# Queries and keys turned on TensorE in 64x64 array tiles in place of DMA transposes

## The chip, the cores and the metric

The kernel runs on one core of one Trainium2 chip, in one launch. The metric is the device time in microseconds (us) of one execution; the comparison uses the median of several runs. Each kernel also has one profiled execution, whose span is counted from the first to the last instruction of the program.

## The reference

An attention with normalised queries and keys, and behind it a chain of matrix products on its output. In short:

```python
# q, k, v: (8, 12, 448, 64) float32; g_q, g_k: (64,)
q_n = q / sqrt(mean(q * q) + 1e-6) * g_q        # over the last axis; k likewise with g_k
s   = (q_n @ k_n.T) / sqrt(64)
s   = s - max(s)
p   = exp(s); p = p / (sum(p) + 1e-9)
x   = (p @ v), as 3584 tokens x 768             # 8 batches x 448 tokens, 12 heads x 64
a   = x @ w1; b = x @ w2                        # w1, w2: 768 x 1024
out = ((a * b) @ w3) @ w_out                    # w3: 1024 x 1024, w_out: 1024 x 768
```

## The kernel before

**Tiling.** The work is cut into 24 *quads*: a quad is four heads of one batch, so three quads make a batch. Tokens are split as 64 x 7, so that a loaded tile has 128 partitions (two groups of 64 rows) and seven blocks `j` on the free axis. `w3 @ w_out` is formed once on the chip (`w34s`), so the chain behind the attention has two stages: FFN1 (`x` times `w1` and `w2`, multiplied together) and FFN2 (times `w34s`).

**One quad, in order.** `load_qk` brings queries and keys in (L384). `plan_prep` squares them on ScalarE (L487), sums the squares on VectorE (L492), takes the inverse root on ScalarE (L501 and L504) and scales them into the bf16 tile `qks` on VectorE (L526). Then `qks` has to be turned so that the head dimension lies on partitions, into `qkT`. That is done in two ways:

- For the first five quads (`N_PE_T = 5`) `do_turn` transposes the seven 128x128 blocks of one operand on TensorE (L1163) into one PSUM bank, and a copy on VectorE or ScalarE brings them to `qkT`; for queries the copy also multiplies by the gains `g_col`.
- For the 19 quads after these, `send` issues one DMA transpose for each operand on SP's queue (L600). When the queries have landed, VectorE multiplies them by the gains in place (`by_g`, L534).

`do_score` then multiplies keys and queries in 64x64 array tiles (L716), seven scores a quad of four matmuls each, every one followed by an exponential on ScalarE (L738). When two quads are complete their sums and values are formed together (`start_pv`; L782 for the left-over rows in 64x32 tiles, L803 for the rest in 128x32 tiles), and VectorE multiplies by the reciprocal of the sums (L845). Single quads take a longer form of the same. When three quads of a batch are done, the batch's FFN pairs join a list of waiting work. A pair (`do_pass`, L908) fills two PSUM banks with sums in 64x64 tiles, one pass of four matmuls at a time, and is emptied by VectorE or ScalarE. Half way through, the row halves of the array exchange banks; a nop on POOL or SP (`hand_over`, L892) stands between the halves. The last token tile is done in `do_last` (L1104).

**What sets the order.** The order of the instructions on every engine is computed when the program is built, by a small planner (`Planner`). It holds a list of jobs with estimated durations and needs, a model of the two DMA queues, and the time at which each PSUM bank comes free (`bank_at`). `pe_try` picks what TensorE does next: a value group, a turn (`any_turn`), a score, the running pair or a new one. Its thresholds are the constants at the top of the kernel (`PAIRS`, `MARGINS`, `LOWS`, `SOONS`, `STOCKS`, `PACES`, `AGAINST` and others; where there are two values, the second holds from `SWITCH = 55.0` on). On the chip the engines are kept in step by semaphores alone: the planner's times decide the order, not when something runs.

**Tile shapes.** The 64x64 tiles of scores and passes, the 128x128 of turns, the 64x32 and 128x32 of values are different settings of the array. The planner charges a change between them `DRAIN = 0.11` us (`into`).

**The start.** `WARM = 15` matmuls on an empty tile run while the first data arrive (L1360), and the planner fills TensorE's idle time up to `WARM_TO` with smaller ones (L1233).

Of the kernel before, what the change touches and what calls it, by code (L numbers as in the profile page):

```python
# [20 lines left out]
SEM = 0.05  # L21
# [5 lines left out]
AFTER = 0.7  # L27
LATE = 0.619
BUSY = 75.0

# [15 lines left out]
class Planner:  # L46
# [50 lines left out]
    def commit(self, job, start, engine):  # L97
        end = start + job.took[engine]
        self.free[engine] = end
        end += LAG[engine]  # L100
        self.jobs.remove(job)
        job.at = start
        if job.any:
            job.emit(engine)
        else:
            job.emit()
        if job.moves is not None:
            work, piece = job.moves
            ticket = [INF]
            self.landed[engine].append(ticket)  # L110

            def landed(t):
                self.note(job, t, engine)
                t += LATE if t > BUSY else 0.0
                ticket[0] = t
                if job.done:
                    job.done(t)

            self.moving[engine].append([start + AHEAD[engine], work, landed, piece])
        elif job.done:  # L120
            job.done(end)
# [74 lines left out]
def kernel(  # L196
# [41 lines left out]

    N_PE_T = 5
    QUAD = 13.122  # L240
    WARM = 15
    WARM_TO = 13.215
    WARM_N = 256
    PAIRS = (2, 3)
    MARGINS = (0.267, 0.281)
    LOWS = (0, 2)
    VALUE_BANKS = (6, 6)
    HOLD = 0
    SOONS = (2, 4)
    STARVES = (6, 5)  # L250
    HUNGERS = (0.632, 0.85)
    ONES = (0, 0)
# [4 lines left out]
    EARLY = 4  # L257
    STOCKS = (17, 14)
    PACES = (1.289, 1.754)
    SWITCH = 55.0  # L260
    LONGEST_SEND = 3.0
    SPLIT = 1
    SQUARE_ON_DVE = ([0, 0],)
    SCALE_ON_ACT = ()
    LATER = 12.232
    BY_G = 0.36
    KEYS = (1.8, 1.348)
    AGAINST = (68, 115, 120, 138, 154, 245, 257, 272, 278, 299, 308, 326)
    POOL_ORDER = (
# [5 lines left out]
    THIN_FROM = 9  # L275
    THIN = 0.627
    QUIET = 0.2

# [110 lines left out]
    def plan_load_qk(i, key=None):  # L389
        eng, queue = (nc.gpsimd, "POOL") if i in ON_POOL else (nc.sync, "SP")  # L390

        def thin():

            left = sum(x[1] for x in plan.moving["SP"])
            return 0.0 if i < THIN_FROM or left < THIN else INF

        parts = 2 if i in IN_PARTS else 1
        for which in range(2):
            got = []

            def done(t, which=which, got=got):
                got.append(t)
                landed[i]["qk"[which]] = all_of(got, parts)

            for n in range(parts):
                x0, x1 = 2 * n // parts, 2 * (n + 1) // parts
                add(
                    queue, {"SP": 0.4, "POOL": 0.75}[queue],
                    (quad(i) - 30 if key is None else key) + which * 0.01 + n * 0.001,
                    lambda which=which, x0=x0, x1=x1: load_qk(i, which, eng, x0, x1),  # L410
                    needs=[lambda: qk_free[i % 3] + (1.0 if i > 5 else 0.0), thin],
                    done=done, moves=(1.35 / parts, 0.086),
                )
# [19 lines left out]
    def plan_load_v(i, key, pieces=range(4)):  # L433
# [13 lines left out]
        for z in pieces:  # L447
            add(
                "POOL", 0.62, key + z * 0.01, lambda z=z: load_v(i, z),
                needs=[lambda: v_free[i % 4] + (3.0 if i > 3 else 0.0), quiet], done=done,  # L450
                moves=((0.46, 0.06), (0.38, 0.05))[z % 2],
            )
# [21 lines left out]
    def plan_prep(i):  # L474
        s = st[i]
        pe = i < N_PE_T
        key = quad(i)
# [54 lines left out]

        def by_g():
            nc.vector.tensor_scalar(  # L534
                out=s["qkT"][:, 0], in0=s["qkT"][:, 0], scalar1=g_col, scalar2=None,
                op0=MULT,
            )

        alpha_at = [INF, INF]
# [44 lines left out]

        def sent(t):
            def done(z):
                s["sent"][t] = z
                if t:
                    put(qkT_at[i], t)(z)
                else:  # L590
                    add(
                        "DVE", BY_G, key - 8, by_g, needs=[lambda: z + SEM],
                        done=put(qkT_at[i], t),
                    )

            return done

        def send(t):
            sent_at[0] = plan.now
            nc.sync.dma_start_transpose(  # L600
                out=s["qkT"][:, t], in_=s["qks"][:, t].rearrange("p j x d -> p (j x d)")
            )

        def complete(t, z):
            scaled_at[i][t] = z + SEM
            if max(scaled_at[i]) < INF and i + 3 < NQ:
                if i + 3 not in ON_POOL:
                    plan_load_qk(i + 3)
                plan_prep(i + 3)
            if not pe:  # L610
                add(
                    "SP", 1.3, key - 8 + t, lambda: send(t),
                    needs=[lambda: scaled_at[i][t]],
                    done=sent(t), moves=(1.6, 0.026),
                )

# [241 lines left out]
    pairs = []  # L858
    sent_at = [0.0]
    waiting = []  # L860
# [23 lines left out]
    def hand_over(p, mm, t):  # L884

        at = t + 0.23
        e = "POOL"
        if max(w_at["w2"]) == INF or (
            max(free["SP"], sent_at[0] + LONGEST_SEND) <= at and plan.moving["POOL"]
        ):  # L890
            e = "SP"
# [143 lines left out]
    def ffn2_pair(bp, t):  # L1035
        def evacuate(p, at):
# [13 lines left out]
            def copied(e):  # L1050
                freed(z)(e)
                for x in range(2):
                    if x and bp == B // 2 - 1:
# [6 lines left out]
                        "SP", 0.57, -20.0, lambda x=x: store(x),  # L1060
                        needs=[lambda: e + SEM], moves=(0.55, 0.14),
                    )
# [89 lines left out]

    turns = [(i, w) for i in range(N_PE_T) for w in range(2)]
    w3_turns = list(range(CF))

    def do_turn(t, i, w, z):
        s = st[i]
        ps = ps_all[:, z, :].bitcast(BF)[:, 0 : NJ * NP].rearrange(
            "p (j s) -> p j s", j=NJ
        )  # L1160
        took = into("t") + NJ * 0.067
        for j in range(NJ):
            nc.tensor.transpose(  # L1163
                ps[:, j], s["qks"][:, w, j].rearrange("p x d -> p (x d)"), ident
            )
        bank_at[z] = INF
        at = t + took + 0.18
        s["sent"][w] = at

        def done(e):  # L1170
            bank_at[z] = e + SEM
            qkT_at[i][w] = e

        add(
            None, {"DVE": 0.53, "ACT": 0.83}, -950.0 + i,
            lambda e: copy_on(e, s["qkT"][:, w], ps, None if w else g_col),
            needs=[lambda: at, lambda: consts_at["g"]], done=done,
# [30 lines left out]
    def any_turn(t, r, idle, n):  # L1208
# [3 lines left out]
        if turns:  # L1212
            i, w = turns[0]
            if scaled_at[i][w] <= r:
                turns.pop(0)
                return do_turn(t, i, w, single(idle))
        ready = [fc for fc in w3_turns if w_at["w3"][fc] + SEM <= r]
# [124 lines left out]
    with tc.manual_schedule():  # L1342
# [39 lines left out]

        warm(WARM)
        free.update(ACT=4.0, DVE=4.0, SP=4.0, POOL=2.3, PE=7.2)
        plan.now = plan.moved_to = 2.2
# [15 lines left out]
        def weight(emit, moves, done):  # L1401
            add("POOL", 0.6, -100.0 + seq[0], emit, done=done, moves=moves)

# [49 lines left out]
```

## Time and profile before

| | |
|---|---|
| median of three runs | 351.32 us (350.1 to 352.6) |
| the profiled execution | 349.81 us, of which the span is 348.0 us |
| granted TensorE clock, mean | 0.998 |
| TensorE busy | 342.3 us (98%), 7373 matmuls |
| TensorE weight loads busy | 219.3 us (63%) |
| VectorE busy | 206.7 us (59%) |
| ScalarE busy | 260.8 us (75%) |
| DMA transposes | 38 on SP's queue, median 4.0 us from issue to landing |
| gain passes at L534 | 19, 8.7 us together |
| turns at L1163 | 70 matmuls of 128x128 |

"PE" in the profile is TensorE's matmuls, "PEld" its weight loads, "DVE" VectorE, "ACT" ScalarE, "POOL" GpSimd and "SP" the engine that issues most DMAs. Matmuls are pipelined: one instruction's time is longer than the distance to the next one's start, so a busy TensorE is not a full one. The distance between starts tells what it is able to do. "Idle before" in the groups is the time that an engine stood still just before these instructions, and what ended it.

### The profile page before, as it was taken

The page shows a single profiled execution, that of the slowest core. Times are in us where ns is not written, and L with a number is a line of the kernel's source. Part 1 is how long each engine was busy: PE and PEld are TensorE (multiplying, and loading weights), DVE is VectorE, ACT ScalarE, POOL GpSimd, SP SyncE. Part 2 cuts the span into 40 slices and gives each one's busy share as a digit, 9 for nine tenths or more (in the row PEclk, how much of TensorE's full clock was granted, in tenths as well). Part 3 has the DMA queues.
Part 4 walks back from the last instruction along what each step waited for, and adds up shares of the span by engine and source line. Part 5 has one row for each costly group of instructions (what it writes and reads, how often), then busy time and mean ns, then how long its engine had stood idle before and what let it go on. Part 6 is the DMA issues. An engine that isn't in the chain of part 4 may idle for free.

```text
span 348.0 us, 16174 instructions
## 1 busy us (share of the span) xinstructions
PE 342.3 (98%) x7373; PEld 219.3 (63%) x7373; DVE 206.7 (59%) x296; ACT 260.8 (75%) x371; POOL 76.9 (22%) x134
## 2 busy tenths in 40 slices
PE   8999999999999999999999999999999999999995
PEld 4767756656775756566666575566665665666674
DVE  5369289898956687486567963865894313222100
ACT  4779989999997997998799797978987882222122
POOL 8556820302222301222022022212204000000000
PEclk9999999999999999999999999999999999999999
DMA  8999999499995969948898699477898051000055
GB/s 197 206 312 204 241 299 268 89 202 199 208 187 174 92 156 188 260 107 154 148 246 161 169 165 259 116 131 186 197 185 105 7 133 53 4 2 2 4 166 155
DMA packets 68488, 55.11 MB, mean 158 GB/s; under 512 B 45060, under 2 KB 62372, under 8 KB 68420
## 3 DMA queue, kind: packets, MB, share of 16 engines
q1 hardware_dynamic: 49440, 35.33, 43.0%
q0 software_dynamic: 18048, 16.92, 29.6%
q10 hardware_dynamic: 932, 1.84, 1.4%
q8 instruction: 57, 0.93, 1.1%
q14 instruction: 11, 0.09, 0.1%
HBM read 46.66 MB, written 11.01 MB: 166 GB/s over the span
## 4 chain that ended last, share of the span: by engine, by line
PE 98%; ACT 1%; DVE 0%; issue 0%
PE ps_all L908 68%; PE ps_all L803 13%; PE ps_all L716 9%; PE ps_all L782 2%; PE ps_all L1360 2%; PE ps_all L1163 1%; PE ps_all L1185 1%; PE ps_all L1104 1%; PE ps_all L1233 1%; ACT P L738 0%; DVE abT L989 0%; ACT qk_sb L369 0%; DVE warm_t L1343 0%; PE ps_all L1373 0%
## 5 line engine op out<-in xcount | busy, mean ns | idle before, releaser
L738 ACT ACTIVATE P<-ps_all 128x896 bf16<-128x896 f32 x114 | 99.5, 916 | 11.7 <-PE ps_all L716 10.8
L424 POOL DMA_DIRECT2D v_sb<-in_v_dram x96 | 57.3, 611 | 184.1 <-PE ps_all L716 120.3
L908 PE MATMUL ps_all<-xT,w2s 64*64 64x448 bf16 x1536 | 88.5, 349 | 0.0
L908 PE MATMUL ps_all<-xT,w1s 64*64 64x448 bf16 x1536 | 86.5, 349 | 0.0
L908 PE MATMUL ps_all<-w34s,abT 64*64 64x384 bf16 x1728 | 80.2, 323 | 0.4 <-DVE abT L989 0.4
L369 ACT ACTIVATE half<-ps_all 128x896 bf16<-128x896 f32 (+1 forms) x35 | 30.6, 874 | 48.5 <-PE ps_all L908 48.3
L908 PEld LDWEIGHTS <-abT 64*64 64x64 bf16 x1728 | 51.7, 107 | 20.3 <-issue 0.7
L908 PEld LDWEIGHTS <-w2s 64*64 64x64 bf16 x1536 | 46.5, 107 | 25.6
L908 PEld LDWEIGHTS <-w1s 64*64 64x64 bf16 x1536 | 46.0, 107 | 25.7 <-issue 0.4
L716 PE MATMUL ps_all<-qkT 64*64 64x448 bf16 x672 | 60.3, 351 | 0.0
L989 DVE TENSOR_TENSOR abT<-ps_all,half 128x896 bf16<-128x896 f32 x32 | 34.8, 1089 | 41.2 <-PE ps_all L908 41.1
L492 DVE TENSOR_REDUCE ssq<-sq 128x14 f32<-128x896 f32 (+1 forms) x50 | 51.2, 1041 | 12.5 <-ACT sq L487 12.2
L526 DVE TENSOR_TENSOR qks<-qk_sb,al 128x448 bf16<-128x448 f32 x96 | 54.6, 616 | 4.8 <-ACT al L504 4.7
L487 ACT ACTIVATE sq<-qk_sb 128x896 f32<-128x896 f32 (+1 forms) x50 | 45.1, 917 | 1.6 <-DMA qk_sb<-in_q_dram 1.3
L845 DVE TENSOR_TENSOR xT<-ps_all,r 128x448 bf16<-128x448 f32 x48 | 27.5, 618 | 25.6 <-ACT r L826 22.0
L716 PEld LDWEIGHTS <-qkT 64*64 64x64 bf16 x672 | 21.7, 106 | 13.2 <-issue 4.2
L908 PE MATMUL ps_all<-w_outs,w3T 64*64 64x384 bf16 x512 | 25.1, 324 | 0.1
L803 PE MATMUL ps_all<-P,v_sb 128*32 128x448 bf16 x456 | 25.0, 352 | 0.0
L738 ACT ACTIVATE w_outs<-ps_all 128x896 bf16<-128x896 f32 x24 | 21.4, 915 | 3.2 <-PE ps_all L716 3.0
L803 PEld LDWEIGHTS <-v_sb 128*32 128x32 bf16 x592 | 15.9, 97 | 12.2 <-issue 0.2
L738 ACT ACTIVATE Pr<-ps_all 128x896 bf16<-128x896 f32 x24 | 22.1, 920 | 0.6 <-PE ps_all L716 0.5
L375 DVE COPY half<-ps_all 128x768 f32<-128x768 f32 x13 | 12.4, 955 | 12.7 <-PE ps_all L908 12.7
(63 smaller groups left out, 210.9 us busy)
## 6 DMA issues: line engine op xcount, KB each, us to landing
out_dram<-half SPq DMA_DIRECT2D x48, 192.0 KB, 3.3
qk_sb<-in_q_dram SPq DMA_DIRECT2D x15, 448.0 KB, 6.3
qk_sb<-in_k_dram SPq DMA_DIRECT2D x15, 448.0 KB, 5.4
v_sb<-in_v_dram POOLq DMA_DIRECT2D x48, 64.0 KB, 4.0
v_sb<-in_v_dram POOLq DMA_DIRECT2D x48, 48.0 KB, 4.1
qk_sb<-in_q_dram POOLq DMA_DIRECT2D x5, 448.0 KB, 8.7
qk_sb<-in_k_dram POOLq DMA_DIRECT2D x5, 448.0 KB, 9.4
w3s<-in_moe_w_dram POOLq DMA_DIRECT2D x8, 256.0 KB, 6.8
```

What stands on the lines that cost most here:

```text
L369: nc.scalar.activation(out=out, in_=in_, func=AF.Copy, scale=1.0 if by is None else by)
L375: nc.vector.tensor_copy(out=out, in_=in_)
L424: nc.gpsimd.dma_start(out=v_bufs[i % 4][p0 : p0 + HP, g::2, 0 : j1 - j0].rearrange("p h j d -> p h (j d)"), in_=src[:, g::2, j0:j1].rearra ...
L487: nc.scalar.activation(out=out, in_=in_, func=AF.Square)
L492: nc.vector.tensor_reduce(out=s["ssq"][:, t, x0:x1], in_=s["sq", t][:, x0:x1], axis=AX, op=ADD)
L526: nc.vector.tensor_tensor(out=s["qks"][:, t, :, x], in0=src[:, t, x], in1=s["alpha"][:, t, x].unsqueeze(2).broadcast_to([NP, NJ, D]), op=MULT,
L716: nc.tensor.matmul(out=sc[HP * c : HP * c + HP, u, 0:S].rearrange("p (j s) -> p j s", j=NJ), lhsT=qkT[u * D : (u + 1) * D, 1, j, cols], rh ...
L738: lambda: nc.scalar.activation(out=dst, in_=sc[:, :, 0:S], func=AF.Exp),
L803: nc.tensor.matmul(out=ps_all[hd * HALF : (hd + 1) * HALF, z, 0:S], lhsT=value_weights(i, hd, j, kind), rhs=s["P"][:, hd, j, :] if j < NF ...
L845: lambda: nc.vector.tensor_tensor(out=xT[b][:, 2 * m + kind - 1, :], in0=ps, in1=s["r"], op=MULT),
L908: mm = nc.tensor.matmul(out=ps_all[64 * h : 64 * h + 64, p.bank + z, 0 : p.n], lhsT=lhsT[64 * r : 64 * r + 64, 64 * h : 64 * h + 64], rhs= ...
L989: nc.vector.tensor_tensor(out=abT[bp][:, f0 : f0 + 2, odd * S : (odd + 1) * S], in0=ps_all[:, z : z + 2, 0:S], in1=a_sb[b, f0], op=MULT,)
```

## The change

Every quad's operands are turned on TensorE. The first five quads (`SMALL_FROM = 5`, the same five) keep the 128x128 turn into one bank. The 19 after these take a turn in 64x64 array tiles: each 128x128 block is transposed as four 64x64 quarters, one on each tile of the array. The two row halves write to two adjacent banks, so the turn asks for a pair of free banks (`adjacent`), and the copy to `qkT` puts the halves together again. `send`, `sent` and `by_g` go: the gains come with the copy. A turn in 64x64 tiles counts as the mode of passes and scores in the planner, so it charges no change of shape for it, and `TURN = 0.036` us for each of the seven blocks.

```diff
-    N_PE_T = 5
+    SMALL_FROM = 5
+    TURN = 0.036
...
-    turns = [(i, w) for i in range(N_PE_T) for w in range(2)]
+    turns = [(i, w) for i in range(NQ) for w in range(2)]
...
     def do_turn(t, i, w, z):
         s = st[i]
-        ps = ps_all[:, z, :].bitcast(BF)[:, 0 : NJ * NP].rearrange(
-            "p (j s) -> p j s", j=NJ
-        )
-        took = into("t") + NJ * 0.067
+        small = i >= SMALL_FROM
+        banks = (z, z + 1) if small else (z,)
+        dst = s["qkT"][:, w]
+        if small:
+            ps = ps_all[:, z : z + 2, :].bitcast(BF)[:, :, 0 : NJ * HP].rearrange(
+                "p r (j s) -> p r j s", j=NJ
+            )
+            dst = dst.rearrange("p j (r s) -> p r j s", r=2)
+            took = into("n") + NJ * TURN
+        else:
+            ps = ps_all[:, z, :].bitcast(BF)[:, 0 : NJ * NP].rearrange(
+                "p (j s) -> p j s", j=NJ
+            )
+            took = into("t") + NJ * 0.067
         for j in range(NJ):
-            nc.tensor.transpose(
-                ps[:, j], s["qks"][:, w, j].rearrange("p x d -> p (x d)"), ident
-            )
-        bank_at[z] = INF
+            block = s["qks"][:, w, j].rearrange("p x d -> p (x d)")
+            if not small:
+                nc.tensor.transpose(ps[:, j], block, ident)
+                continue
+            for r in range(2):
+                rows = slice(HP * r, HP * r + HP)
+                for c in range(2):
+                    nc.tensor.transpose(
+                        ps[HP * c : HP * c + HP, r, j],
+                        block[rows, HP * c : HP * c + HP],
+                        ident[rows, rows],
+                        tile_position=(HP * r, HP * c),
+                    )
+        for x in banks:
+            bank_at[x] = INF
...
         add(
             None, {"DVE": 0.53, "ACT": 0.83}, -950.0 + i,
-            lambda e: copy_on(e, s["qkT"][:, w], ps, None if w else g_col),
+            lambda e: copy_on(e, dst, ps, None if w else g_col),
             needs=[lambda: at, lambda: consts_at["g"]], done=done,
         )
...
-        def by_g():
-            nc.vector.tensor_scalar(
-                out=s["qkT"][:, 0], in0=s["qkT"][:, 0], scalar1=g_col, scalar2=None,
-                op0=MULT,
-            )
...
-        def send(t):
-            sent_at[0] = plan.now
-            nc.sync.dma_start_transpose(
-                out=s["qkT"][:, t], in_=s["qks"][:, t].rearrange("p j x d -> p (j x d)")
-            )
...
         if turns:
             i, w = turns[0]
-            if scaled_at[i][w] <= r:
+            z = single(idle) if i < SMALL_FROM else adjacent(idle)
+            if scaled_at[i][w] <= r and z is not None:
                 turns.pop(0)
-                return do_turn(t, i, w, single(idle))
+                return do_turn(t, i, w, z)
```

The later order is planned anew: the second values of the thresholds change, with some constants of the DMA model (one lateness for each kind of transfer in place of one for all) and the numbers of the warm matmuls. `hand_over` no longer allows for a DMA transpose being sent on SP. Loads and stores keep their queues.

```diff
-LATE = 0.619
-BUSY = 75.0
+LATES = {'qk': 1.35, 'v': -0.44, 't': 2.08, 's': 2.04, 'w': 0.619}
+BUSY = 68.73
...
-    WARM = 15
+    WARM = 12
...
-    PAIRS = (2, 3)
-    MARGINS = (0.267, 0.281)
-    LOWS = (0, 2)
+    PAIRS = (2, 2)
+    MARGINS = (0.267, 0.237)
+    LOWS = (0, 0)
...
-    SOONS = (2, 4)
-    STARVES = (6, 5)
-    HUNGERS = (0.632, 0.85)
+    SOONS = (2, 1)
+    STARVES = (6, 6)
+    HUNGERS = (0.632, 1.144)
...
-    STOCKS = (17, 14)
-    PACES = (1.289, 1.754)
+    STOCKS = (17, 16)
+    PACES = (1.289, 1.58)
...
-    LATER = 12.232
-    BY_G = 0.36
-    KEYS = (1.8, 1.348)
-    AGAINST = (68, 115, 120, 138, 154, 245, 257, 272, 278, 299, 308, 326)
+    LATER = 13.076
+    KEYS = (1.8, 1.262)
+    AGAINST = (83, 99, 123, 136, 157, 199)
...
-        if max(w_at["w2"]) == INF or (
-            max(free["SP"], sent_at[0] + LONGEST_SEND) <= at and plan.moving["POOL"]
-        ):
+        if max(w_at["w2"]) == INF or free["SP"] <= at and plan.moving["POOL"]:
...
-        free.update(ACT=4.0, DVE=4.0, SP=4.0, POOL=2.3, PE=7.2)
+        free.update(ACT=4.0, DVE=4.0, SP=4.0, POOL=2.3, PE=7.85)
```

More of the change, by code (lines that the diff above doesn't have):

```diff
@@ L107, in commit @@
         if job.moves is not None:
-            work, piece = job.moves
+            work, piece, kind = job.moves
             ticket = [INF]
@@ L113, in landed @@
                 self.note(job, t, engine)
-                t += LATE if t > BUSY else 0.0
+                t += LATES[kind] if t > BUSY else 0.0
                 ticket[0] = t
@@ L257 @@
     EARLY = 4
-    STOCKS = (17, 14)
-    PACES = (1.289, 1.754)
+    STOCKS = (17, 16)
+    PACES = (1.289, 1.58)
     SWITCH = 55.0
-    LONGEST_SEND = 3.0
     SPLIT = 1
@@ L275 @@
     THIN_FROM = 9
-    THIN = 0.627
-    QUIET = 0.2
+    THIN = 0.3
+    QUIET = 0.1
     w1s = const.tile([128, CM, DFF], BF, name="w1s")
@@ L411, in plan_load_qk @@
                     needs=[lambda: qk_free[i % 3] + (1.0 if i > 5 else 0.0), thin],
-                    done=done, moves=(1.35 / parts, 0.086),
+                    done=done, moves=(1.35 / parts, 0.086, "qk"),
                 )
@@ L450, in plan_load_v @@
                 needs=[lambda: v_free[i % 4] + (3.0 if i > 3 else 0.0), quiet], done=done,
-                moves=((0.46, 0.06), (0.38, 0.05))[z % 2],
+                moves=((0.46, 0.06, "v"), (0.38, 0.05, "v"))[z % 2],
             )
@@ L475, in plan_prep @@
         s = st[i]
-        pe = i < N_PE_T
         key = quad(i)
@@ L583, in plan_prep @@
             )
[L585 to L593, printed above, removed]
-                    )
-            return done
-        def send(t):
-            sent_at[0] = plan.now
-            nc.sync.dma_start_transpose(
-                out=s["qkT"][:, t], in_=s["qks"][:, t].rearrange("p j x d -> p (j x d)")
-            )
         def complete(t, z):
@@ L609, in complete @@
                 plan_prep(i + 3)
[L610 to L614, printed above, removed]
-                )
         def scaled(t):
@@ L858 @@
     pairs = []
-    sent_at = [0.0]
     waiting = []
@@ L1060, in copied @@
                         "SP", 0.57, -20.0, lambda x=x: store(x),
-                        needs=[lambda: e + SEM], moves=(0.55, 0.14),
+                        needs=[lambda: e + SEM], moves=(0.55, 0.14, "s"),
                     )
@@ L1157, in do_turn @@
         s = st[i]
-        ps = ps_all[:, z, :].bitcast(BF)[:, 0 : NJ * NP].rearrange(
-            "p (j s) -> p j s", j=NJ
-        )
-        took = into("t") + NJ * 0.067
-        for j in range(NJ):
-            nc.tensor.transpose(
-                ps[:, j], s["qks"][:, w, j].rearrange("p x d -> p (x d)"), ident
-            )
-        bank_at[z] = INF
+        small = i >= SMALL_FROM
[12 more added lines that the diff above has]
+            took = into("t") + NJ * 0.067
+        for j in range(NJ):
+            block = s["qks"][:, w, j].rearrange("p x d -> p (x d)")
[13 more added lines that the diff above has]
+            bank_at[x] = INF
         at = t + took + 0.18
@@ L1170, in done @@
         def done(e):
-            bank_at[z] = e + SEM
+            for x in banks:
+                bank_at[x] = e + SEM
             qkT_at[i][w] = e
@@ L1401, in weight @@
         def weight(emit, moves, done):
-            add("POOL", 0.6, -100.0 + seq[0], emit, done=done, moves=moves)
+            add("POOL", 0.6, -100.0 + seq[0], emit, done=done, moves=(*moves, "w"))
         for name in POOL_ORDER:
```

## The prediction

> **What bounds the kernel now.** I read the page's spans and busy times first, then the chain that ended last, then TensorE's own waits, and last a table of stretches.
>
> ```profile
> span 348.0 us, 16174 instructions
> ...
> PE 342.3 (98%) x7373; PEld 219.3 (63%) x7373; DVE 206.7 (59%) x296; ACT 260.8 (75%) x371; POOL 76.9 (22%) x134
> ...
> PE 98%; ACT 1%; DVE 0%; issue 0%
> ```
>
> The chain is TensorE from end to end. A busy TensorE need not be a full one, because its matmuls are pipelined, so I looked for what it waits on and for the pitch at which its work starts:
>
> ```profile
> PE ps_all L1360 <- DVE warm_t L1343: 1.2, 1, 1.2
> PE ps_all L908 <- DVE abT L989: 0.4, 1, 0.4
> ```
>
> ```profile
> 25.24 0.39 PE ps_all L1163 x7
> ...
> 28.37 0.50 PE ps_all L1163 x7
> ...
> 155.31 1.89 PE ps_all L908 x40
> ...
> 341.34 2.78 PE ps_all L1104 x64
> ```
>
> The first fence is the whole list of TensorE's waits (total, times, longest): one before the work begins and one of 0.4 us. The second is the chain in order of time (start, us, line, matmuls). Ten passes of four 64x64 tiles over 448 columns take 1.89 us, 189 ns each. Seven 128x128 turns over 128 columns take 0.39 us, 56 ns each. The last tile's 32 pairs over 192 columns take 2.78 us, 83 ns each after one change of tile shape. All three are columns / 2.4 + 2.5 ns, a full clock (0.998 granted). The turn at 28.37 took 0.11 us more than that at 25.24 because TensorE came from another tile shape: a change of shape costs 0.11 us.
>
> From the counts in the page I rebuild what TensorE must do. FFN passes over 448 columns: 3072/4 = 768 x 0.189 = 145.2. Passes over 384: (1728 + 512)/4 = 560 x 0.1625 = 91.0. Scores: 672/4 = 168 x 0.189 = 31.8. Values: 888/4 = 222 and 264/8 = 33, together 255 x 0.189 = 48.2. Turns: (70 + 64) x 0.056 = 7.5. Last tile: 2.7. Sum 326.4 us. The first turn starts at 8.3 and the last matmul ends at 344.1, 335.8 us; about 1.1 of that is filler on the warm tile. So only 8.3 us is lost in the whole run, and the timeline has 54 changes of tile shape, 54 x 0.11 = 5.9 us. **True stalls are about 2.4 us.** There is almost nothing idle to put new work into.
>
> ```profile
> 55.00:165.00 110.00, 109.56 (x2386) 71.00 (x2378) 83.92 (x118) 100.10 (x144) 22.91 (x39) 1.00 0.87 174
> 165.00:275.00 110.00, 110.00 (x2448) 68.13 (x2440) 75.54 (x106) 91.99 (x129) 22.33 (x38) 1.00 0.83 164
> ```
>
> The columns are PE, PEld, DVE, ACT and POOL busy. Here, where the change falls, ScalarE is busy 192.1 of 220 us and VectorE 159.5; neither is full.
>
> **The added turns.** 19 quads x 2 operands x 7 blocks = 266 blocks, each of four 64x64 transposes (four loads, four matmuls over 64 columns). No row shows a 64-column matmul. Below, the pitch law gives 64/2.4 + 2.5 = 29.2 ns a block, if the four tiles run side by side as the score tiles do (their starts lie 3 to 4 ns apart): 266 x 29.2 = 7.8 us. Above, the 128x128 turn's 56 ns, which is also what a block costs if its weight load is not hidden (27 + 29): 14.9 us. Where between, the loads say:
>
> ```profile
> L908 PEld LDWEIGHTS <-w2s 64*64 64x64 bf16 x1536 | 46.5, 107 | 25.6
> L782 PEld LDWEIGHTS <-v_sb 64*32 64x32 bf16 x176 | 2.6, 91 | 0.6
> ```
>
> 32 more columns cost 107 - 91 = 16 ns, 0.5 ns a column, so a tile's 64 columns take 32 ns to load, a little over the 27 ns of streaming that should cover them. The 128x128 turns keep the matmul law's pitch with a load in front of each, so loads do run under matmuls. I take the load as the limit, 32 + 2.5 = 34.5 ns: **266 x 34.5 = 9.2 us**. (The plan in the change charges 36 ns, near to this; it is no measurement of this trace.) Passes and scores use 64x64 tiles too, so no change of shape is added for these turns.
>
> The Trainium skill, "TensorE: Matmul & The Clock Gate", section "LDWEIGHTS (loading the stationary operand)", puts a load at columns / 1.2 ns, 53 ns for 64 columns, and "TensorEngine Tiling (Array Packing)", "Gotcha 2: Feature Incompatibilities", says that column tiling rules out fast weight load, so that nothing would shorten it. By that rule, an estimate, the blocks would be bound by 53 ns and cost 14.2 us; the difference of the two load rows above speaks for 0.5 ns a column against the rule's 0.83, and no run here shows the load at full rate. The first page's section "Back-to-back issue gap" also has a floor of about 25 ns a matmul; were it to hold across tiles, a block would be 100 ns and the sum 26.6 us, but starts 3 to 4 ns apart in the trace contradict it for different tiles.
>
> **The waits that come with them.** Each turn's first load waits in TensorE's queue for VectorE's scaled operand, and everything on TensorE is queued behind it. The plan issues a turn when it believes the operand is ready; where it is later, TensorE stands. The ten old turns show the price: PEld L1163 waited for DVE 0.8 + 0.3 us, 0.11 us a turn. Over 38 turns that is 0 to 4.2 us; the old turns sit in the crowded start, so I take 1.0. Against it the new order may lose fewer of the 2.4 us of true stalls: 0 to -2.4, I take -0.5.
>
> **The copies.** Each turn ends in a copy out of PSUM. The rows: 620 ns (DVE), 675 with the gain (DVE), 918 and about 1000 (ACT). On VectorE 19 x (0.62 + 0.675) = 24.6 us, on ScalarE 36.5, less the 19 gain passes removed at L534, 8.7. The two engines hold 351.6 of 440 us between 55 and 275; after, 367 to 379 of about 460: 80 to 83%. Cost on the path nothing: the cover is TensorE's passes, of which the plan keeps up to 16 in stock. Without the cover a score waits for turn, copy and semaphores, about 1.1 us, shorter than the 4.0 us landing and 0.45 us gain pass that it replaces. Each turn holds two banks for that 1.1 us, 84 bank-us of some 1800 in that stretch, and the plan has two pairs in flight where it had three; I price this at nothing, and as a rival.
>
> **What is removed.** 38 DMA transposes on SP's queue (1.26 us issue, 4.0 us to land) and the gain passes. TensorE never waits for either, so they return nothing: nothing on the chain of waits names them. SP's queue stands less (L600 waits 57.2 us for qks in it), which frees hand-over nops and stores behind it; TensorE's 0.4 us says that nothing there was late. Loads of q, k and v keep their queues; only their order is planned anew.
>
> **The start.** Three warm matmuls fewer, six fillers fewer. VectorE's second scaling of queries ends at 8.23 and the first turn's matmul starts at 8.29, so the data set that time, and nothing is gained. Should the clock fall in the gap, a microsecond at half speed costs about half of one; I put 0. The number of paired (11) and single (2) value groups cannot shrink: 24 quads, the first alone.
>
> **The sum.** 348.0 + 9.2 + 1.0 - 0.5 = 357.7 us of span. The profiled execution took 349.8 for its 348.0; the median of the runs is 351.3, 1.5 above that. The same 9.7 us on the median: **361.0 us**, 2.8% more. Changes under 1% (3.5 us) can't be told from none here: the runs before lie between 350.1 and 352.6.
>
> **Rivals.**
> 1. *Loads not hidden.* A block costs 56 ns: 14.9 + 0.5 on the median, 366.7. For it: no row has loads this dense, 56 loads and matmuls in a quarter microsecond. Against it: the 0.5 ns a column. 0.12.
> 2. *A new stall takes over*: turns too early for their operand, or a pair waiting for banks that a turn holds. At the old 0.11 us a turn 4.2, with the turns 9.2: 364.7 with nothing won back. For it: TensorE is in order, and 38 new waits stand in its queue. Against it: TensorE waited 0.4 us in all under the old plan. 0.13.
> 3. *Not slower.* The new order packs the lost 8.3 us away while blocks cost the least, 29.2 ns. It decides where losses fall by over 4.3 us (7.8 - 3.5), below 4.0; all stalls gone and a few changes of shape too. With 5.0 won back, 351.3 + 7.8 - 5.0 = 354.1. Against it: 5.9 of the 8.3 are changes of shape from turns and value groups that stay. 0.04.
> The forecast itself has 0.71, its own range 357.5 to 363.5.
>
> **How the numbers follow.** The least that the work allows is +7.8 - 2.4 = 5.4, 356.7; the most, +14.9 + 4.2, 370.4, needs two rivals at once. I give 356.5 to 367.0. All cases but the third are slower by over 1%: slower 0.96, same 0.03, faster 0.01.
>
> **What would show it.** Right: TensorE still ends the chain at 97% or more; 1064 more matmuls; seven blocks in about 0.24 us between passes; load rows of L1163's successor near 107 ns; VectorE and ScalarE together up 16 to 28 us; no DMA transposes; the first turn still at about 8.3. Wrong: blocks at 50 ns or more (rival 1), PEld waits on DVE of several microseconds or idle TensorE between 70 and 270 (rival 2), fewer than 45 changes of shape (rival 3).

## The result, and the profile after

| | before | after |
|---|---|---|
| median | 350.76 us (4 runs, 350.1 to 352.6) | 369.54 us (4 runs, 367.0 to 373.8) |
| profiled execution, its span | 349.8, 348.0 us | 369.7, 367.8 us |
| ratio | | 1.050, 95% interval 1.043 to 1.058 |

By the medians the change costs 18.8 us. The ratio compares the means of the fast runs alone and leaves out one slow run after, 373.8 us: 17.6 us, 5.0%. The direction was as forecast; the size is about twice the 9.7 us of the sum and lies above the range, if just under the 370.4 us that the prediction named as the most. The page after, its span, its busy times and the engines of the chain that ended last:

```profile
span 367.8 us, 18242 instructions
...
PE 354.2 (96%) x8428; PEld 234.1 (64%) x8428; DVE 211.0 (57%) x298; ACT 275.8 (75%) x388; POOL 76.7 (21%) x134
...
PE 81%; ACT 10%; DVE 4%; issue 2%; DMA 1%; DVEq 0%
```

TensorE ended 98% of the chain before and 81% now. Its own list of waits (total, times, longest) is no longer two lines; the longest entries:

```profile
PE ps_all L872 <- issue: 2.4, 2, 1.7
PE ps_all L749 <- DVE qkT L372: 1.6, 4, 0.4
PE ps_all L1349 <- DVE warm_t L1332: 1.2, 1, 1.2
PE ps_all L749 <- DVE qkT L374: 1.2, 1, 1.2
PE ps_all L1141 <- DVE qks L524: 0.6, 1, 0.6
...
```

L749 is the value group, and it waits for the *copies of turns* (`qkT`, L372 and L374). It does not read `qkT`: it needs the banks that the copies empty. L872 is a pass of the FFN that stands for "issue", that is, for nothing that the profile shows.

The turns themselves, by groups (busy us, mean ns of one, idle before) and in the chain in order of time (start, us, line, matmuls):

```profile
L1146 PEld LDWEIGHTS <-qks 64*64 64x64 bf16 x1064 | 15.0, 108 | 4.3 <-issue 0.8 <-DVE qks L524 0.5
L1146 PE MATMUL ps_all<-ident,qks 64*64 64x64 bf16 x1064 | 14.8, 193 | 0.5 <-ACT P L705 0.4
```

```profile
181.07 1.30 PE ps_all L872 x32
182.37 0.22 PE ps_all L1146 x28
182.59 0.76 PE ps_all L872 x16
183.35 0.19 PE ps_all L683 x4
```

A turn of seven blocks between two stretches of passes takes 0.22 us, 31 ns a block, and 38 of them 8.4 us. The two stretches, columns as before:

```profile
55.00:165.00 110.00, 103.49 (x2655) 70.13 (x2651) 87.36 (x122) 102.07 (x149) 21.93 (x37) 1.00 0.63 151
165.00:275.00 110.00, 109.50 (x2835) 71.82 (x2831) 71.82 (x100) 93.41 (x127) 21.99 (x37) 1.00 0.47 104
```

The second is almost as full as before, the first is not. I took the starts of all TensorE instructions from the trace, gave each its pitch (189 ns a pass, 31 a block, and so on) and called the rest dead. After the first turn, before lost 8.4 us and after 19.2; in both, 5.9 of it are the 54 changes of tile shape that the prediction counted.

| stretch, us | before | after | idle turns in before's order (below) | new thresholds alone (below) |
|---|---|---|---|---|
| 8 to 68 | 3.2 | 3.5 | 3.1 | 3.0 |
| 68 to 100 | 0.7 | 4.7 | 1.1 | 9.1 |
| 100 to 130 | 1.5 | 5.1 | 2.4 | 0.7 |
| 130 to 175 | 0.7 | 2.6 | 0.6 | 1.5 |
| 175 to the end | 2.3 | 3.3 | 2.6 | 2.9 |

The last matmul ends 19.0 us later: 8.4 of array time and 10.8 of dead time make 19.2. Of the stops over 0.14 us past 60 us, 3.6 us end with a turn's copy on VectorE, 2.6 with a result of ScalarE, 2.8 with nothing shown, and about 1.1 with others (in before: 0.2 with a result of ScalarE, 0.6 with others). A stop for a copy, in the timeline (start, us, engine, instruction, in brackets the idle time before it and its releaser), and the chain that leads to it:

```profile
70.00 0.62 PE L1146 MATMUL ps_all<-ident,qks 64*64 64x64 bf16 x56
70.53 0.68 DVE L372 TENSOR_SCALAR qkT<-ps_all,g_col 128x896 bf16<-128x896 bf16 x1
71.13 0.61 DVE L374 COPY qkT<-ps_all 128x896 bf16<-128x896 bf16 x1
71.80 0.38 PE L749 MATMUL ps_all<-Pr,ones 64*32 64x448 bf16 x8 [1.17 <-DVE qkT L374]
```

```profile
67.37 1.00 DVE abT L953
68.37 1.07 DVE qks L524 x2
69.44 1.00 DVE ssq L490
...
70.53 0.21 DVE qkT L372
70.74 0.39 issue
71.13 0.62 DVE qkT L374
...
71.80 0.35 PE ps_all L749
```

Two turns in a row (56 matmuls) hold four banks, VectorE empties them one after the other, and a value group stands behind. From 60 to 72 us the chain lies on ScalarE and VectorE. Before, it was passes and scores alone there, with the value group right behind them:

```profile
70.52 0.19 PE ps_all L716 x4
70.71 1.32 PE ps_all L908 x28
72.04 0.69 PE ps_all L782 x24
```

### The profile page after: what moved, and what is told of

The parts are those of the page before. It is cut to its first block, busy times and chain, and to the rows that moved or that the text cites. A ratio compares the mean times of both kernels' runs of the same rounds, so it can differ in the third digit from the quotient of the medians.

```text
span 367.8 us, 18242 instructions
## 1 busy us (share of the span) xinstructions
PE 354.2 (96%) x8428; PEld 234.1 (64%) x8428; DVE 211.0 (57%) x298; ACT 275.8 (75%) x388; POOL 76.7 (21%) x134
## 4 chain that ended last, share of the span: by engine, by line
PE 81%; ACT 10%; DVE 4%; issue 2%; DMA 1%; DVEq 0%
PE ps_all L872 56%; PE ps_all L770 11%; PE ps_all L683 7%; ACT P L705 4%; PE ps_all L1146 2%; PE ps_all L749 2%; ACT sq L485 2%; ACT half L368 1%; DVE abT L953 1%; PE ps_all L1141 1%; DVE ssq L490 1%; DVE qkT L372 1%; PE ps_all L1173 1%; DMA qk_sb<-in_q_dram 1%; PE ps_all L1068 1%
## 5 line engine op out<-in xcount | busy, mean ns | idle before, releaser
L705 ACT ACTIVATE P<-ps_all 128x896 bf16<-128x896 f32 x114 | 100.7, 917 | 12.4 <-PE ps_all L683 11.0
L872 PE MATMUL ps_all<-xT,w1s 64*64 64x448 bf16 x1536 | 89.2, 349 | 1.7 <-issue 1.7
L872 PE MATMUL ps_all<-xT,w2s 64*64 64x448 bf16 x1536 | 89.6, 350 | 0.8 <-issue 0.7
L872 PE MATMUL ps_all<-w34s,abT 64*64 64x384 bf16 x1728 | 80.0, 323 | 0.1
L368 ACT ACTIVATE half<-ps_all 128x896 bf16<-128x896 f32 (+1 forms) x39 | 33.5, 866 | 49.9 <-PE ps_all L872 49.8
L872 PEld LDWEIGHTS <-abT 64*64 64x64 bf16 x1728 | 54.2, 107 | 17.2 <-issue 1.1
L872 PEld LDWEIGHTS <-w1s 64*64 64x64 bf16 x1536 | 46.9, 107 | 25.3 <-issue 2.1
L872 PEld LDWEIGHTS <-w2s 64*64 64x64 bf16 x1536 | 46.4, 107 | 25.9 <-issue 1.6
L683 PE MATMUL ps_all<-qkT 64*64 64x448 bf16 x672 | 62.1, 351 | 0.2 <-ACT P L705 0.2
L683 PEld LDWEIGHTS <-qkT 64*64 64x64 bf16 x672 | 22.9, 106 | 12.7 <-issue 4.0
L872 PE MATMUL ps_all<-w_outs,w3T 64*64 64x384 bf16 x512 | 25.1, 324 | 0.1
L872 PEld LDWEIGHTS <-w3T 64*64 64x64 bf16 x512 | 15.4, 107 | 6.1 <-issue 0.7
```

The source lines that it names most:

```text
L368: nc.scalar.activation(out=out, in_=in_, func=AF.Copy, scale=1.0 if by is None else by)
L683: nc.tensor.matmul(out=sc[HP * c : HP * c + HP, u, 0:S].rearrange("p (j s) -> p j s", j=NJ), lhsT=qkT[u * D : (u + 1) * D, 1, j, cols], rh ...
L705: lambda: nc.scalar.activation(out=dst, in_=sc[:, :, 0:S], func=AF.Exp),
L872: mm = nc.tensor.matmul(out=ps_all[64 * h : 64 * h + 64, p.bank + z, 0 : p.n], lhsT=lhsT[64 * r : 64 * r + 64, 64 * h : 64 * h + 64], rhs= ...
```

## The experiments

Each was timed against the kernel before on the same chip; a number in brackets is the 95% interval of the ratio. Each paragraph says what its run tells apart, whatever letters the expectation uses for the theories.

**What the array time costs.** To before, 38 small turns are added whose results nobody uses: one ahead of each of the first two scores of a quad past the fifth, written to the two banks that this score fills next. No copy, no bank and no order is touched. In the second kernel they stand ahead of the first four scores, twice as many.

```diff
         qkT, sc = s["qkT"], ps_all[:, z : z + 2]
+        if i >= N_PE_T and g < 2:      # g < 4 in the second
+            spare = ...
+            for j in range(NJ):
+                block = s["qks"][:, g % 2, j].rearrange("p x d -> p (x d)")
+                ...  four nc.tensor.transpose into spare, as in the change
```

> The kernel before, with the 38 turns added as idle work: ahead of the first two scores of each quad past the fifth, TensorE makes the 28 transposes of one operand in 64x64 tiles into the score's own two banks, which the score then overwrites. Nobody reads them; the order, the DMA transposes, the copies and the banks stay those of before. Theory A (a turn costs its array time, some 0.22 us, and the rest of the loss is waiting that the new order brings): 38 x 0.22 = 8.4 us more than before, span 356 to 357, ratio 1.024. Theory B (TensorE runs out of fetched instructions, since 56 of them go in a quarter microsecond): 8.4 and some 1 to 3 us of stops without any wait, ratio 1.027 to 1.033. Theory C (the true price of a turn is twice its pitch, in any order): about 19 us, ratio 1.054.

> As the run with idle turns, but ahead of the first four scores of each quad, 76 idle turns. Theory A: twice as much, 16.8 us over before, ratio 1.048. Theory B: more than twice as much, since the stops come where bursts are dense: 20 us or more, ratio 1.057 and up. Theory C: about 38 us, ratio 1.11.

Measured 360.27 us, 1.028 (1.025 to 1.031): +9.5. In the profile 8.4 are array time and 1.4 two stops for "issue". The forecast's term for turns was 9.2; that it comes so near is in part luck, since it had no stops in it. Twice as many cost 380.9, 1.086 (1.076 to 1.095). These four runs lie in two pairs, 377.7 and 378.1, and 383.7 and 384.2. The profiled execution is of the lower pair, so I go by that: +27, not 19, of which 16.8 are array time, 9 us stops for "issue", and one or two I did not trace. What the upper pair lost its 6 us to is not known. What the stops are comes below.

**128x128 turns instead.** `SMALL_FROM = 24` in after.

> The changed kernel with all quads turned as 128x128 blocks into one bank, planned by the same constants. A turn takes 14 instructions in place of 56, one bank in place of two, but 0.39 us of array time and two changes of shape, 0.22: 0.61 against 0.22 us. Theory A (array time): 38 x 0.39 = 15 us more than the changed kernel where turns stand alone, some 12 where two stand together, 381 to 385. Theory B (instruction fetch): its 2.8 us of stops are gone, 379 to 382. Theory E (the waits come from turns that hold two banks each): several microseconds less than these, 375 to 379.

377.47 us, 1.075 (1.072 to 1.077), 7.9 us over after. The 64x64 tiles are the cheaper form, by 8 us in 38 turns, with the order planned anew in each. Array time and changes of shape (107 in place of 54) alone would have made 12 us or more; the measured time lies where the expectation put it if turns that hold one bank in place of two save some microseconds. No run here tells banks from order in this.

**Cutting turns and copies in after.** The turns past the fifth quad transpose one block of seven (the copy reads this block seven times and stays as long as it was), or the copy takes one block of seven (scores read that block for all), or both. The edit of both, without that of the scores:

```diff
-        for j in range(NJ):
+        for j in range(1 if small else NJ):
...
-            lambda e: copy_on(e, dst, ps, None if w else g_col),
+            lambda e: copy_on(
+                e, *((dst[:, :, 0:1], ps[:, :, 0:1]) if small else (dst, ps)),
+                None if w else g_col,
+            ),
```

> The changed kernel in its own order, with one block of seven transposed in each of the 38 small turns; the copy reads that block seven times, so it is as long as it was and banks are held as long. The scores get wrong operands of the right shape. Theory A: the array time of six blocks goes, 38 x 6 x 0.0315 = 7.2 us, 369.5 becomes 362.3, and the waits stay. Theory B: the 2.8 us of stops without a wait go too, 359.5. If another engine than TensorE sets the pace behind the waits, less comes back than 7.2: 364 or more.

> The changed kernel in its own order, turns in full, but the copy out of PSUM takes one block of seven, about 0.2 us in place of 0.62 to 1.0; scores use that block for all seven. The two banks of a turn come free sooner, and VectorE and ScalarE have 38 short instructions in place of long ones. Theory A: the waits of value groups and passes on those copies (1.3, 0.6, 0.5, 0.6, 0.5 us at the profile's five longest, all in front of value groups) go, 4 to 7 us: 363 to 366. Theories B and C: at most 1 us, 368.5 to 369.5.

> The changed kernel in its own order, with one block of seven transposed in each small turn, and the copy of that block alone (scores use it for all seven). The two cuts alone brought 5.2 us (turns) and 4.1 us (copies) against the 369.5 of the changed kernel. Theory A (array time and waits on copies are separate costs): they add up, 9.3 us, 360.2. Theory D (between 68 and 175 us ScalarE and VectorE set the pace together with TensorE, so that what one gives back the other takes): the sum is more than the parts only if copies were the other side of the turns, 357 or less; if the exponentials of ScalarE are the other side (97% busy from 68 to 130 with the turns cut), still about 360 to 362, and waits of TensorE on ScalarE stay.

Turns cut: 364.31, 1.039 (1.036 to 1.041), -5.2 against after: 7.1 us of array time and the stops for "issue" are gone, but other waits grew. Copies cut: 365.45, 1.042 (1.038 to 1.046), -4.1; TensorE's waits on `qkT` copies fall from 3.6 to 1.4 us. Both: 360.68, 1.029 (1.026 to 1.032), -8.9, near the sum of the two. **With a seventh of turn and copy left, 10 us over before remain**, 1.2 of them the array time of the 38 blocks that are left. I put the rest down to the order, as what remains when turns and copies are taken away; no run changes the order of this kernel and nothing else. Where TensorE stops in it, by its starts as above: 4.5 us end with a result of ScalarE, against 0.2 in before, and about 1 with a turn's copy.

**The order alone.** The second of these two kernels is before with the thresholds of after (`PAIRS`, `MARGINS`, `LOWS`, `SOONS`, `STARVES`, `HUNGERS`, `STOCKS`, `PACES`, `LATER`, `KEYS`, `AGAINST`, `THIN`, `QUIET`), DMA transposes kept; the first is after with those of before. The constants of the DMA model stay in each as they were; they too are part of the new order, and no run tests them alone.

> The changed kernel with the later thresholds of before (PAIRS, MARGINS, LOWS, SOONS, STARVES, HUNGERS, STOCKS, PACES, LATER, KEYS, AGAINST, THIN, QUIET): real turns, and the order planned by before's choices. Theory F as first said (the new thresholds are the price of the waits): it should come near the run with idle turns, 360 to 364. Theory G (each set of thresholds is fitted to its own work, and the waits come from the work that turns bring with them, whatever the set): slower than the changed kernel, 371 to 378.

> The kernel before, DMA transposes and all, with the changed kernel's later thresholds (PAIRS, MARGINS, LOWS, SOONS, STARVES, HUNGERS, STOCKS, PACES, LATER, KEYS, AGAINST, THIN, QUIET) and nothing else of the change. Theory F (the new order, made for turns, is itself the price of the waits): 5 to 9 us over before, 356 to 360. Theories A, D and E (the turns, their copies or their banks make the waits): within 2 us of before, 349 to 353.

New thresholds alone: 359.29, 1.025 (1.023 to 1.028), **+8.6 us with no instruction added**. Turns with the old thresholds: 374.26, 1.063 (1.060 to 1.067), 4.7 worse than after. The chain with the new thresholds alone, in order of time:

```profile
84.89 1.79 PE ps_all L908 x44
86.68 0.21 PE ps_all L716 x4
...
86.92 2.54 ACT P L738 x3
...
92.69 1.63 ACT w_outs L738 x2
...
94.94 5.15 PE ps_all L803 x62
100.09 0.50 PE ps_all L716 x8
100.59 0.18 PE ps_all L908 x2
```

TensorE's list of waits there:

```profile
PE ps_all L716 <- ACT P L738: 1.7, 5, 0.4
PE ps_all L782 <- ACT w_outs L738: 1.7, 2, 1.2
```

From 88.6 to 100.4 us TensorE's timeline holds no pass, which I read as an empty stock of FFN work, and TensorE stands behind ScalarE's exponentials (L738; the tile `w_outs` serves as a third buffer for them). What lost 0.7 us between 68 and 100 us before now loses 9.1. In the whole run, stops that end with a result of ScalarE are 5.2 us, as in the kernel with turns and copies cut they were 4.5.

**Which part of the turn counts.** After with DMA transposes and gain passes put back for the operands: once with the turns and their copies into a spare tile that nobody reads, once with the turns but no copies.

> The changed kernel with real turns, copies and banks as planned, but each copy goes to a tile that nobody reads, and the scores use operands that come by DMA transpose and gain pass as before (both are issued). Theory G1 (TensorE's waits come from the resources: array time, copies, banks): no gain, 368 to 372. Theory G2 (they come from the chain, scores waiting for their own quad's turn and copy): 4 to 7 us back, 363 to 366.

> As the turns for nobody, but without the copies: a turn's two banks come free when its last matmul is done. The order is planned with the turns' array time and the changed kernel's thresholds. Against the kernel before with the new thresholds (359.3) it adds 38 turns. Theory G1: 359.3 + 8.4 and up to 3 of fetch stops if the new order's waits stay beside the turns, 366 to 371; if the turns fill the waits that the new thresholds leave (9 us between 68 and 100), 360 to 363.

Turns for nobody: 372.86, 1.061 (1.056 to 1.066), no better than after. So it is not the operands' way through turn and copy that costs; banks, engines and order are enough. TensorE still waits 2.7 us for copies to the spare tile. Without copies: 369.70, 1.052 (1.046 to 1.058), as after; 8.6 us of its dead time lie between 68 and 100 us, where the new thresholds alone have their hole too. Put together (medians, us):

| | old thresholds | new thresholds |
|---|---|---|
| no turns past the fifth quad | 350.8 | 359.3 |
| their array time only | 360.3 | 369.7 |
| turns with banks and copies | 374.3 | 369.5 |

Down the first step: 9.5 and 10.4, near the array time and its stops in either order. Down the second: 14.0 with the old thresholds, nothing with the new. But the steps are not alike. The idle turns keep the order of before, while the three other kernels with turns were planned with them; and the 369.7 is of a kernel that still has its DMA transposes and gain passes. With these kept, copies and banks cost 3.2 us (369.7 to 372.9). The 14.0 are not banks and copies alone either: in that run 8.9 us of dead time lie between 68 and 100 us, where TensorE has no pass for 10.4 us. What is shown is that each set of thresholds is the better one for its own work (350.8 against 359.3 without the turns, 369.5 against 374.3 with them), and that one column's parts can't be read as the other's.

**A single threshold?** Before forms one value group alone, `83.27 2.39 PE ps_all L803 x48` in its chain; after has none there but a pair at 90.43. `LOWS` allows it. Before with `LOWS` (0, 0), and before with all new thresholds but `LOWS` (0, 2):

> The kernel before with one threshold changed, LOWS (0, 2) to (0, 0): no quad's values are formed alone to refill the stock of FFN work. The kernel before has one such single value group at 83.3 us; the changed kernel, and before with all new thresholds, do not. Theory S (its absence is most of the 8.6 us that the new thresholds cost): 5 to 8 us over before, 356 to 359, TensorE standing between 85 and 100. Theory M (many thresholds together, each fitted to its own work): 1 to 3 us, 352 to 354.

> The kernel before with all new thresholds but LOWS, which keeps (0, 2). Theory S: most of the 8.6 us comes back, 351 to 354, and the 9 us lost between 68 and 100 fall to 1 or 2. Theory M: the loss between 68 and 100 falls but comes up elsewhere, 357 to 361.

355.26, 1.011 (1.008 to 1.015): this threshold alone costs 4.0 by the medians (in its profiled execution 1.2 of it are two early stops of the kind told below, so the threshold's share may be nearer 3). But given back among the new ones it returns nothing: 360.36, 1.025 (1.020 to 1.029), and TensorE then waits 1.7 us for a pair's product (at 121 us) and 1.6 for a gain pass (at 200). Between 68 and 100 us it loses 2.8 in place of 9.1, after 175 us 6.4 in place of 2.9. The thresholds count together; this one does not carry the loss, and the others were not tested one by one.

**Another plan for after** (`MARGINS` 0.19, `LOWS` 1, `VALUE_BANKS` 4, `HUNGERS` 0.695 as second values).

> The changed kernel with four thresholds set otherwise (MARGINS 0.19, LOWS 1, HUNGERS 0.695, and a value group may start with four free banks in place of six), turns, copies and all else as they are. Theory G (waits come with the work, but the order decides how many): the value groups no longer wait for the banks of the last turns, 2 to 4 us back, 365.5 to 367.5. If the waits were ScalarE's alone (D): within 1 us of 369.5.

367.95, 1.047 (1.042 to 1.052). The interval overlaps that of after, so 1.6 us is no shown gain.

**Is it ScalarE's time?** A theory of mine that fell. ScalarE was busy 102 of 110 us in the first stretch. Squaring one block of seven past the fifth quad takes 22 us off its work in the whole run (275.8 to 254.1 in after), 13 of them in this stretch; the same was done in before as a control.

```diff
-                nc.scalar.activation(out=out, in_=in_, func=AF.Square)
+                cut = slice(0, 1) if i >= 5 else slice(0, NJ)
+                nc.scalar.activation(
+                    out=out[:, :, cut], in_=in_[:, :, cut], func=AF.Square
+                )
```

> The changed kernel in its own order, with ScalarE relieved: from the sixth quad on it squares one block of seven (about 0.2 us in place of 0.92, 38 times, 27 us in all), and VectorE sums that block seven times, as long as before. The norms are wrong; turns, copies, banks and order stay. Theory D (between 55 and 130 us ScalarE, 93 to 96% busy, sets the pace and TensorE waits for it or for what comes after it): 5 to 8 us come back, 361 to 364. Theory H (the waits are for banks that copies hold and for the turns' places in the order, not for ScalarE's time): at most 2 us, 367.5 to 369.5.

> The same relief of ScalarE in the kernel before, as a control: there TensorE loses 2 us between 68 and 130 us. Theories D and H both: 349.5 to 351, at most 1.2 us less than before.

After: 369.10, 1.048 (1.041 to 1.055): not the 5 to 8 us of the theory, and no gain that these runs (366.0 to 370.3) can tell, with the same waits as without the cut (1.5 and 1.2 us on `qkT` copies). Before: 351.38, 1.001 (0.997 to 1.004). ScalarE's amount of work does not set the pace. When it does a thing can matter all the same. The idle turns with 17 us of ScalarE work that the plan knows nothing of (a copy of 896 columns behind each gain pass):

> The kernel before with the 38 idle turns of the first run, and with each of the 19 gain passes one more ScalarE instruction of 128x896 that reads a weight tile and writes a tile that nobody reads, about 0.9 us, 17 us together: near what the changed kernel adds to ScalarE and VectorE (15.0 and 4.3 us busy). Banks and order stay. Theory D (ScalarE's load makes TensorE wait): 3 to 8 us over the run with idle turns (360.3), 363 to 368. Theory A or E (banks held, or the order): at most 1.5 us over it, 360 to 362.

365.58, 1.044 (1.040 to 1.048), 5.3 over the idle turns alone. Its profile has 3 us of stops for "issue" before the first small turn, but the profiled execution was the slowest of the four, 368.2, and the others may lack them; the load costs between 2 and 5 us. This run decides little.

**The stops for "issue".** In after there are two long ones (start, us, what):

```profile
105.71 1.68 PE ps_all L872 x33
107.39 1.70 issue
109.09 0.79 PE ps_all L872 x13
...
112.84 0.22 PE ps_all L1146 x19
...
113.13 0.79 issue
```

Counting TensorE's instructions from the start, loads, matmuls and the few of its sequencer, each long stop without a wait falls at 449 + 256 k (from the traces, by my count):

```
kernel              last start   distance   instruction   k
after                 107.04      2.05 us        4545     16
after                 112.94      0.98           4801     17
idle turns             85.26      0.54           3521     12
idle turns            111.17      1.21           4801     17
idle turns twice       80.07      0.86           3265     11
idle turns twice       85.06      1.24           3521     12
idle turns twice      269.54      1.79          14017     53
padded start          109.24      0.80           4801     17
```

The nine further such stops over 0.3 us with idle turns twice fall there too. The page lists the queue that brings instructions (packets, MB, share):

```profile
q8 instruction: 66, 1.08, 1.2%
```

66 packets of 16 KB for 16,869 instructions of TensorE are one packet for each 256, 64 bytes an instruction. In after one lands at 107.67 us and TensorE goes on at 109.09; the next at 112.50 and it goes on at 113.92: 1.42 us each, and 1.3 to 1.5 at all stops of the table. Passes use some 42 instructions a microsecond (8 in 189 ns), a turn 56 in 0.22 us. To tell a count from a place in the work, 64 tiny matmuls (128 instructions) go ahead of everything in after:

> The changed kernel with 64 matmuls of one column behind the warm matmuls, where TensorE otherwise waits for data: 128 more instructions in front of everything, and the same order after them. Theory B (TensorE runs dry at multiples of 256 instructions, at counts 4545 and 4801 in the changed kernel's profile, 2.8 us): the stops without a wait fall again on 449 + 256 k in the count, which is 128 instructions earlier in the work, so the two at 107 and 113 us do not come at the same place; time 366.5 to 371, by how many bursts now meet a late fetch. Rival (something at that place of the program, not the count, stops it): the two stops stay at the same matmuls, 369.5.

The stop at 4545 is gone, and one is left, again at 4801, which is now 128 instructions earlier in the work:

```profile
108.48 1.10 PE L872 MATMUL ps_all<-xT,w2s 64*64 64x448 bf16 x17
110.04 0.38 PE L872 MATMUL ps_all<-xT,w2s 64*64 64x448 bf16 x4 [0.45 <-issue]
```

The place goes with the count: TensorE ran out of instructions. The time hardly moved, 368.18, 1.049 (1.043 to 1.055), as the stops are 2.8 us in all. Why the packet that landed at 107.67 set out only at 106.71, six instructions before the end, stays open; such stops also came in some runs at counts 1473 and 1729 (43 and 49 us), before the first small turn, 0.3 and 0.8 us even in a kernel that has no small turn (before with the squares cut).

## Why the prediction was wrong in size

- **"266 x 34.5 = 9.2 us": right.** 31 ns a block, 8.4 us; with the fetch stops 9.5 in before's order. The 31 ns lie between streaming alone, 29.2, and the load's 34.5, so whether the load binds is not shown. Nor does the 0.5 ns a column, which came from two rows, go through a third one of before: the 128 columns of a 128x128 turn's load take 98 ns (L1163), less than 64 columns here. Load rows of 108 ns as foretold. The two rules of the Trainium skill that it weighed ("TensorE: Matmul & The Clock Gate", "LDWEIGHTS (loading the stationary operand)" and "Back-to-back issue gap") put a block at 53 and 100 ns; 31 ns shows neither to bind four tiles side by side. Rival 1, 56 ns, is out.
- **"the new order may lose fewer ... I take -0.5": the step that failed.** In the sum, all that is not array time came to +0.5 us: 1.0 of waits, -0.5 for the order, nothing for copies and banks. Measured, the dead time rose by 10.8. The order was taken to be able only to win, because the change called it planned anew. Its thresholds cost 8.6 us when they are given to the old operations, and nearly 9 beside the array time remain when turns and copies are cut from after. That these two are one and the same loss is not shown: the first has a hole at 88 to 100 us that after does not have; in both kernels TensorE stops mostly for results of ScalarE. I read thresholds as a free choice; they are a fit to one set of durations and needs, and before's fit was within 2.4 us of having no stall. That does not make the new ones a bad choice: with the turns they are 4.7 us better than the old.
- **"Cost on the path nothing: the cover is TensorE's passes": failed too.** The averages of 80 to 83% over 220 us hid 68 to 130 us, where TensorE's dead time rose from 2.2 to 9.8, 2.8 of it stops for "issue". In after, 4.1 us go with the copies. With the old thresholds, banks, copies and the order planned around them cost 14.0 over the idle turns. An empty stock of passes is what I read in the run with the new thresholds alone; in after no stretch without a pass is longer than 6.5 us (4.7 in before), so there TensorE stops at a few places, the longest at value groups behind turns.
- **"84 bank-us of some 1800 ... I price this at nothing": failed in the same way.** Value groups waited 2.8 us on L372 and L374 in the list of waits, for copies that they never read. Rival 2 named the like, a pair waiting for a turn's banks, and had 4.2 us for its waits: the kind right, the size too small.
- **The waits of turns' loads, "I take 1.0"**: 0.5 us on `qks` at L1146. Half of that, and harmless beside the rest.
- **Instruction fetch** had no term: 2.8 us in after. The trace of before loses no more than about 0.1 us at such a stop past the warm start, but the count of instructions of a turn was there to be worked out.
- **"TensorE still ends the chain at 97% or more": wrong**, 81%, the sign that was to stand for a new stall. 1064 transposes were added, and the page shows 1055 more matmuls (nine warm and filler ones went, three and six). VectorE and ScalarE together rose 19.3 us, within 16 to 28. "The first turn still at about 8.3": it stayed neutral, under a microsecond either way.
- **"faster 0.01, slower 0.96"**: slower, by 1.043 to 1.058. No kernel here beat before: the array time of turns alone is 8.4 us on an engine that had 2.4 us of stalls.

## What to carry to other kernels

An order fitted to a set of costs is part of the kernel's speed: when operations change and the order is made anew, price the order by itself, by giving it to the old operations, before asking what the operations cost. Cover has to be looked for in the narrowest stretch (the stock of work at each time), not in a mean over a hundred microseconds. And where the bounding engine has 2% idle, work moved to it from idle queues costs its array time, as the 38 idle turns did, whatever it saves elsewhere.

## What the hardware showed that I had not expected

- TensorE can run out of instructions. It then stops for 0.3 to 1.9 us at instruction 449 + 256 k and goes on about 1.4 us after a 16 KB packet lands. Bursts of short ones (56 in 0.22 us) make this more frequent: 2 stops and 1.4 us with 38 idle turns, 12 stops and 9 us with 76; 2.8 us in after.
- Four 64x64 tiles take a fresh load each and 64 columns in 31 ns, as against 56 ns for one 128x128 turn.
- A hole in the order can cost twice. With the new thresholds alone, TensorE was busy under half of the time from 90 to 95 us, its longest stop 1.24 us, and then the granted clock (the column after the five engines) was halved:

```profile
93.55 0.38 PE L782 MATMUL ps_all<-Pr,ones 64*32 64x448 bf16 x8 [1.24 <-ACT w_outs L738]
```

```profile
92.00:95.00 3.00, 1.34 (x32) 0.52 (x35) 0.00 (x0) 3.00 (x4) 0.09 (x1) 0.97 1.19 158
95.00:98.00 3.00, 3.00 (x36) 1.26 (x34) 0.45 (x1) 1.83 (x5) 0.00 (x0) 0.50 1.28 242
```

The value group that began at 94.94 took 5.15 us there, and a pair's 72 matmuls took 3.52 in before. "TensorE: Matmul & The Clock Gate", section "What's actually happening", puts the halving after an idle window of about 3.4 us. The rows agree in kind, but here no stop was that long. In the 3.41 us before the clock halved TensorE was busy for 1.3 us. The same came in two more runs, with turns and the old thresholds (busy 1.5 of 3.41 us before it) and with turns without copies (1.8); the half clock lasted 3.41 us in two of the three and 6.83 in the third.
